# Cluster labels from one product per tile, with the halves added on VectorE, and new planner prices for column-tiled products

## The chip, the cores and the metric

The kernel runs on one core of a Trainium2 chip. The metric is the device time of one execution in microseconds (us): the median of the runs. One more execution was taken by the hardware profiler. The engines are called as in the profile: PE (TensorE's products), PEld (its weight loads), DVE (VectorE), ACT (ScalarE), POOL (GpSimd) and SP (SyncE, which issues the DMAs).

## The reference

Clustered attention over 4 batches, 8 heads, 768 positions and 64 dimensions, followed by a feed-forward layer. Each query and each key gets the label of the nearest of 16 centroids of its head (the largest cosine), and a query sees only keys of its own label:

```python
q_assign = np.argmax(np.einsum('bhsd,hcd->bhsc', q_n, c_n), axis=-1)
k_assign = np.argmax(np.einsum('bhsd,hcd->bhsc', k_n, c_n), axis=-1)
mask = q_assign[:, :, :, None] == k_assign[:, :, None, :]
scores = np.where(mask, scale * np.matmul(q, k.transpose(0, 1, 3, 2)), -1000000000.0)
attn = softmax(scores)
x = (attn @ v).transpose(0, 2, 1, 3).reshape(B * S, H * D)
h = x @ w_in
g = np.where(h >= 1, h, np.where(h <= -1, 0.0, (h + 1) ** 2 / 4))
out = g @ w_out
```

The feed-forward layer is 512 to 2048 to 512. All data are float32.

## The kernel before, in words

**Numbers.** To keep float32 accuracy with float16 products, every operand is split into a high and a low half that are both float16. A product of two such operands then takes three products (high with high, high with low, low with high), or, where one operand is stored with both halves side by side along the contraction, fewer. The rows of q and k are such: 64 dimensions with two halves fill the 128 rows of the array, so one weight tile of q or k holds both halves of 128 positions.

**Stages.** The work is cut into 12 units (`NU`): 4 batches (b) by 3 chunks (c) of 256 query positions. Heads go in 4 pairs (hp). Per batch and pair, `kv_load`, `k_scale`, `k_split`, `v_split` and `k_assign` load k and v, split them and find the keys' labels (12 tiles of 128 keys). Per unit, `q_load`, `q_scale`, `q_split`, `q_assign` and `q_pairs` do the same for q (16 tiles). Then `at_scores`, `at_soft` and `at_av` compute the attention of each pair, and `ffn1` and `ffn2` the feed-forward layer of the unit, in 8 slices f of 256 hidden columns. Slices of the weights are prepared in the first part of the kernel (`w_load`, `w_bits`, `w_split`).

**Labels.** `labels` (line 653) multiplies each tile of 128 positions (the weights, `xT[:, i]`) with the 16 centroids of its head. The centroids too are split into two halves, in `cT[:, a]`, so there are two products of 16 columns for each tile, and the second adds onto the first in PSUM: 32 products for a q unit, 24 for a pair of k. Then VectorE, all on that PSUM bank: the maximum over the 16, `is_equal` with it, times `iota`, the maximum again. The callers subtract that maximum: a zero marks the label.

**Memory.** PSUM has two pairs of banks, of which the scores use `pair[0]` alone once the start is over (`early()`: step under `EARLY` = 22), and `ffn2` the other. `bank_a` belongs to `at_av`. The three banks h, i, j go round in a ring (`hid`, `misc`) among `ffn1`, the labels and all small sums.

**Order.** The order of the instructions isn't written out. Each step of a stage calls a `Recorder`, which collects nodes (one instruction, or a group of products) with what they read and write. `price` (line 87) gives each a cost in ns, `turns` (line 119) says which VectorE and GpSimd instructions must not overlap, and `issue` (line 305) plans `ROUNDS` = 80 orders by list scheduling forwards and backwards. Each is replayed by a model of the machine in four phases of the clock gate, and the order with the smallest sum is issued. The steps (`at(step, fn, ...)`, line 1209 on) only set the recording order and first priorities: unit u begins at step 16u, `q_assign` comes 4.5 steps before it, `k_assign` of batch b and pair hp at step 48b + 4hp - 4 (6 before, for the first batch), `v_split` one step before that. So a change of any price can change the order of everything.

**Column-tiled products.** `at_av` (line 978) uses weight tiles of 64 columns, so that two heads share the array: 8 products of 128 columns for the row sums and 36 of 256 for the values, in one group. `price` calls them `half`: `n / 4.8 + 3.5` ns for n columns. Other products are `max(n / 2.4 + 2.5, 24)`.

Of the kernel before, what the change touches and what calls it, by code (L numbers as in the profile page):

```python
# [12 lines left out]
F32 = mybir.dt.float32  # L13
U32 = mybir.dt.uint32
AF = mybir.ActivationFunctionType
ALU = mybir.AluOpType
AX = mybir.AxisListType
# [25 lines left out]

LOOK, MARGIN = 0.4, 4000
ROUNDS = 80

class Recorder:
# [9 lines left out]
    def __init__(self, tc):  # L59
        self.tc, self.nc = tc, tc.nc  # L60
        self.nodes, self.seen, self.open, self.step = [], {}, None, -99
        for name in ("tensor", "scalar", "vector", "gpsimd", "sync"):
            setattr(self, name, Engine(self, name, getattr(tc.nc, name)))

# [22 lines left out]
    def price(self, eng, op, out, ins, kw):  # L87

        if "dma" in op:
            n = 1  # L90
            for k in out.shape:
                n *= k
            kb = n * mybir.dt.size(out.dtype) / 1024

            return 33, 79.0 if kb == 2 else kb, "transpose" in op
        n = max(self.free(a) for a in [out] + ins[:1])
        ps = any(a.space == PSUM for a in ins)
        cols = sum(isinstance(kw.get(k), bass.AP) for k in ("scale", "bias", "scalar", "scalar1", "scalar2"))
        if eng == "tensor":
            n = self.free(ins[1])  # L100
            half = self.free(ins[0]) <= 64 and n > 100
            if ins[1].dtype == F32:
                n *= 4

            return n / 4.8 + 3.5 if half else max(n / 2.4 + 2.5, 24)
        if eng == "scalar":
            cols += kw.get("accum_out") is not None
            first = n == 1 and kw.get("scale") == 0.0

            apart = n > 512 and any(list(a.ap)[-1][0] == 2 and mybir.dt.size(a.dtype) == 4 for a in [out] + ins[:1])  # L110
            return 93 + n / 1.2 + 94 * cols - 43 * ps + 1283 * first + 75 * apart
        if eng == "vector":
            fast = 1
            if op in ("tensor_scalar", "tensor_copy") and not ps:
                fast = 4 if mybir.dt.size(out.dtype) == 2 and mybir.dt.size(ins[0].dtype) == 2 and n > 64 else 2
            return 68 + n / 0.96 / fast + 61 * cols + 20 * (op == "reciprocal")
        return (150 if n < 16 else 55) + n * (2.03 if op == "tensor_tensor" else 0.9 if op == "memset" else 3.5)
# [187 lines left out]
    def issue(self):  # L305
# [4 lines left out]
        best = None  # L310
        for _ in range(ROUNDS):
            self.forward(prio)
# [83 lines left out]
class Group:  # L396
# [8 lines left out]
        r.nodes.append(r.open)  # L405

    def __exit__(self, *a):
        self.rec.open = None


class Engine:
# [22 lines left out]
def view(buf, shape, dtype):  # L434
    n = 1
    for k in shape:
        n *= k
    ap = buf.bitcast(dtype)[:, :n]
    if len(shape) > 1:
        names = "abcd"[: len(shape)]  # L440
        ap = ap.rearrange(
            "p (" + " ".join(names) + ") -> p " + " ".join(names), **dict(zip(names[1:], shape[1:]))
        )
    return ap
# [3 lines left out]
def tile_clustered_attention_moe(  # L448
# [12 lines left out]
    C = cent.shape[1]  # L461
# [5 lines left out]
    T = S // P  # L467
    NP = H // 2
    CT = 2
# [19 lines left out]
    rec = Recorder(tc)  # L489
# [4 lines left out]
    def tiles(name, n, size):  # L494
        return [const.tile([P, size // 4], U32, name=f"{name}{i}") for i in range(n)]

    def new(tag, shape, dtype, n=1):

        if tag not in rings:
            size = mybir.dt.size(dtype)  # L500
            for k in shape:
                size *= k
            rings[tag] = Ring(tiles(tag, n, -(-size // 32) * 32))
        return rings[tag](*shape, dtype=dtype)
# [26 lines left out]
    start = iter([0, 1] * 2).__next__  # L531

    def early():

        return rec.step < EARLY

    def misc(*shape):
        return hid(*shape, dtype=F32)
# [24 lines left out]
    cT = const.tile([P, 2, P], F16, name="cT")  # L563
# [69 lines left out]
    def transpose(out, nat, ps=None):  # L633
        nat = nat.rearrange("p n a d -> p (n a d)")
        if ps is None:
            rec.sync.dma_start_transpose(out=out, in_=nat)
            return

        n = out.shape[1] // 2
        ps = view(ps, [2, 4 * 256], BF16)  # L640
        nat, out = nat.bitcast(BF16), out.bitcast(BF16).rearrange("p (x n) q -> p x (n q)", x=2)
        for x in range(2):
            with rec.group():
                for i in range(n):
                    rec.tensor.transpose(ps[:, x, i * P : (i + 1) * P], nat[:, (x * n + i) * P : (x * n + i + 1) * P], idb)
            rec.scalar.copy(out[:, x], ps[:, x, : n * P])
# [3 lines left out]
        rec.scalar.activation(out=hi, in_=src, func=AF.Copy, scale=sc)  # L650
        rec.vector.scalar_tensor_tensor(out=lo, in0=src, scalar=sc, in1=hi, op0=ALU.mult, op1=ALU.subtract)

    def labels(z1, xT, n, heads):

        with rec.group():
            for i in range(n):
                for a in range(2):
                    h = heads[i]
                    rec.tensor.matmul(
                        z1[:, i], xT[:, i], cT[:, a, h * C : (h + 1) * C], start=(a == 0), stop=(a == 1)  # L660
                    )
        mx = new("mx", [NP * SC], F32)[:, :n]

        def wide(x):
            return x.unsqueeze(2).to_broadcast([P, n, C])

        rec.vector.tensor_reduce(out=mx, in_=z1, op=ALU.max, axis=AX.X)
        rec.vector.tensor_tensor(out=z1, in0=z1, in1=wide(mx), op=ALU.is_equal)
        rec.vector.tensor_tensor(out=z1, in0=z1, in1=iota.unsqueeze(1).to_broadcast([P, n, C]), op=ALU.mult)
        rec.vector.tensor_reduce(out=mx, in_=z1, op=ALU.max, axis=AX.X)  # L670
        return wide(mx)

    def kv_load(b, hp):
        slot = slots[hp]
# [47 lines left out]
    def k_assign(b, hp):  # L722

        e = KV[b, hp]
        n = 2 * T
        z1 = misc(n, C)
        kn = e["kn"]
        mx = labels(z1, e["kT"], n, [2 * hp + i // T for i in range(n)])
        rec.vector.tensor_tensor(out=z1, in0=z1, in1=mx, op=ALU.subtract)
        rec.gpsimd.memset(kn[:, :, 1, C:], 0.0)  # L730
        rec.vector.tensor_scalar(
            out=kn[:, :, 1, :C], in0=z1, scalar1=0.0, scalar2=-ONE, op0=ALU.not_equal, op1=ALU.mult
        )
        e["k1"] = view(e["parts"][1 if b == 0 else 2], [n, P], F16)
        transpose(e["k1"], kn, pair[start()] if b == hp == 0 else None)

        pn = misc(2, C)
        with rec.group():
            for t in range(T):
                rec.tensor.matmul(pn, ones, kn[:, t::T, 1, :C], start=(t == 0), stop=(t == T - 1))  # L740
        rec.vector.tensor_scalar(
            out=BX[b]["has"][:, hp], in0=pn, scalar1=-ONE * (S - 0.5), scalar2=None, op0=ALU.is_gt
        )

    Q = {}
    NQ = NP * SC
# [32 lines left out]

    def q_assign(u):  # L780
        e = Q[u]
        z1 = misc(NQ, C)
        mx = labels(z1, e["qT"], NQ, [i // CT for i in range(NQ)])
        zs = e["z"] = new("zs", [NQ, C], F32)
        rec.vector.tensor_tensor(out=zs, in0=z1, in1=mx, op=ALU.subtract)
        e["er"] = new("er", [NQ], F32, 2)

# [431 lines left out]
    for b in range(B):  # L1219
# [11 lines left out]
        for c in range(NCH):  # L1231
            u = b * NCH + c
            s0 = first(b, 0, c)
            for x, fn in zip((PRO, -9.1, -8.1, -6.1) if u == 0 else (s0 - 14, s0 - 6.8, s0 - 6.4, s0 - 4.5), (q_load, q_scale, q_split, q_assign)):
                at(x, fn, u)
            for hp in range(0, NP, NP if c else 1):
                at(first(b, hp, c) - (5.5 if u == 0 else 3), q_pairs, u, hp, NP if c else 1)
            for hp in range(NP):
                s0 = first(b, hp, c)
                for n in range(SC):  # L1240
                    at(s0 + n, at_scores, b, hp, c, n // CT, n % CT)
                    at(s0 + n + 1, at_soft, b, hp, c, n // CT, n % CT)
                at(s0 + LA - 0.5, at_av, b, hp, c)

            sf = max(sf, s0 + FA)
            G = NF if u else GF
            for f in range(NF):
                if f % G == 0 and (u < 2 or c == 0):
                    if u == 0:
                        sf = max(sf, wat[2 * (f + G) - 1] + 2)  # L1250
                    at(sf - 1, ffn_scale, [u] if u == 0 else range(u, (b + 1) * NCH), range(f, f + G))
                at(sf, ffn1, u, f)
                at(sf + 3, ffn2, u, f)
                sf += 2
    for i in range(2 * NF):
        f, a = divmod(i, 2)
# [47 lines left out]
```

## Time and profile before

| | |
|---|---|
| median of 3 runs | 867.04 us (865.24 to 868.2) |
| the profiled execution: its time | 869.13 us |
| its span, first to last instruction | 867.30 us |
| mean granted clock of TensorE | 0.984 |
| instructions | 19633 |

The profile's page lists, for each engine, its busy time, its share of the span and its number of instructions. The chain that ended last is followed back from the last instruction, at each step to what released it. A group of instructions is a line with engine, operation, out<-in by the program's names (bank numbers and buffer numbers left out), partitions x elements, count, busy us, mean ns of one, and after the bar the idle time of the engine just ahead of them and what ended it. All instructions have the recorder's line 322, so one goes by the names: `cT` are the centroids, `kn` and `n` the natural k, `bankh`, `banki`, `bankj` the ring of banks, `zs` the labels of q, `sS` the scores, `hl` their halves, `r` and `g` the hidden layer. A timeline line is start, length, engine, product or operation, and how many were merged. Products overlap in the array, and their ends are modelled, so the time from start to start is what one costs.

### The profile page before, as it was taken

To read this page: it belongs to the slowest core of one execution; us is meant where nothing else is said; L and a number is where in the kernel's file an instruction comes from. 1 tells how busy PE (TensorE), PEld (TensorE's weight loads), DVE (VectorE), ACT (ScalarE), POOL (GpSimd) and SP (SyncE) were. 2 spreads that over 40 slices of the span, in tenths; PEclk is the share of its full clock that TensorE was granted. 3 is DMA by queue.
4 is the path that set the end of the run, shared out by engine and by line. 5 is a ranking of instruction groups with operands and counts; after the bars stand their busy time and mean duration, and the time that the engine had idled before them with its cause. 6 is when DMAs were issued, how large, how long until landed. Compare 5 with 4: busy or idle time off the path is not lost.

```text
span 867.3 us, 19633 instructions
## 1 busy us (share of the span) xinstructions
PE 809.4 (93%) x7452; PEld 561.1 (65%) x7452; DVE 650.4 (75%) x1485; ACT 637.4 (73%) x1128; POOL 550.1 (63%) x527
## 2 busy tenths in 40 slices
PE   3687559999999999999999999999999999999997
PEld 3454346666767766767666766767667667676664
DVE  7999999998978868678778768678887757544322
ACT  6799888986867778678777687686776687676232
POOL 1166688876756777756766677666667577666222
PEclk9998889999999999999999999999999999999999
DMA  9985689869999979988998978998999787666100
GB/s 315 241 248 146 171 204 204 147 140 162 197 169 199 168 151 177 192 185 190 183 189 173 169 141 173 198 161 167 177 216 162 141 160 131 113 135 109 20 25 25
DMA packets 404767, 142.55 MB, mean 164 GB/s; under 512 B 372800, under 2 KB 396352, under 8 KB 404672
## 3 DMA queue, kind: packets, MB, share of 16 engines
q1 hardware_dynamic: 404672, 141.30, 80.2%
q8 instruction: 58, 0.95, 0.5%
q14 instruction: 37, 0.30, 0.1%
HBM read 40.40 MB, written 6.29 MB: 54 GB/s over the span
## 4 chain that ended last, share of the span: by engine, by line
PE 80%; DVE 12%; ACT 3%; issue 2%; DMA 2%; POOL 0%; ACTq 0%; SPq 0%; DVEq 0%; POOLq 0%
PE pair L322 40%; PE banka L322 11%; PE bankj L322 10%; PE banki L322 9%; PE bankh L322 9%; DVE sS L322 2%; DVE w L322 2%; DVE wk L322 1%; ACT w L322 1%; DMA q<-qn 1%; ACT hl L322 1%; DVE banki L322 1%; DVE qn L322 1%; ACT sS L322 1%; DVE q L322 1%
## 5 line engine op out<-in xcount | busy, mean ns | idle before, releaser
L322 POOL TENSOR_TENSOR hl<-sS,hl 128x768 f16<-128x768 f32 x176 | 299.8, 1711 | 116.0 <-ACT hl L322 83.7
L322 PE MATMUL pair<-w,g 128*128 128x512 f16 x1152 | 271.1, 379 | 0.0
L322 PEld LDWEIGHTS <-w 128*128 128x128 f16 x2304 | 223.4, 98 | 44.3 <-issue 2.6
L322 ACT ACTIVATE sS<-sS,sbi 128x768 f32<-128x768 f32 x192 | 179.3, 934 | 91.9 <-DVE sbi L322 88.6
L322 DVE CUSTOM_DVE_ANT_0 sS<-pair,zero,er 128x768 f32<-128x768 f32 x192 | 194.2, 1011 | 66.4 <-PE pair L322 41.6
L322 PEld LDWEIGHTS <-g 128*128 128x128 f16 x1152 | 110.3, 98 | 116.3 <-issue 1.6
L322 PE MATMUL pair<-kv,q 128*128 128x384 f16 x768 | 160.9, 334 | 17.6 <-DVE sbi L322 9.2
L322 ACT CAST hl<-sS 128x768 f16<-128x768 f32 x176 | 143.8, 825 | 12.9 <-DMA pT<-hl 7.9
L322 POOL TENSOR_TENSOR g<-r,g 128x512 f16<-128x512 f32 x88 | 103.7, 1179 | 63.7 <-ACT g L322 53.8
L322 PEld LDWEIGHTS <-q 128*128 128x128 f16 x1152 | 84.1, 99 | 72.8 <-issue 26.1
L322 PE MATMUL banka<-pT,kv 128*64 128x256 f16 (+1 forms) x1680 | 107.2, 282 | 0.4 <-DMA pT<-hl 0.4
L322 ACT ACTIVATE r<-r,f_ra,f_rs 128x512 f32<-128x512 f32 x88 | 71.3, 811 | 43.3 <-DVE r L322 42.5
L322 PEld LDWEIGHTS <-kv 128*64 128x64 f16 (+1 forms) x1968 | 96.9, 108 | 2.9 <-issue 1.5
L322 ACT CAST g<-r 128x512 f16<-128x512 f32 x88 | 53.8, 611 | 13.1 <-DVE r L322 10.2
L322 PE MATMUL bankh<-x,w 128*128 128x256 f16 x432 | 51.9, 273 | 0.2 <-POOL x L322 0.2
L322 POOL TENSOR_TENSOR qn<-qn,phi 128x256 f16<-128x256 f16 x48 | 34.2, 731 | 27.1 <-DVE phi L322 17.5
L322 PE MATMUL bankj<-x,w 128*128 128x256 f16 x408 | 48.3, 273 | 0.0
L322 PE MATMUL banki<-x,w 128*128 128x256 f16 x312 | 38.0, 273 | 0.0
L322 POOL TENSOR_TENSOR w<-w 128x1024 f16<-128x1024 f32 x12 | 30.2, 2513 | 10.6 <-ACT w L322 9.3
L322 PE MATMUL banki<-wk,w 128*128 128x256 f16 x312 | 36.7, 273 | 0.0
L322 ACT ACTIVATION_READ_ACCUMULATOR sS<-sS,sbi 128x1 f32 x192 | 36.0, 188 | 0.0
L322 PEld LDWEIGHTS <-ones 128*128 128x128 bf16 x256 | 18.0, 105 | 27.2 <-issue 21.6
(238 smaller groups left out, 1069.0 us busy)
## 6 DMA issues: line engine op xcount, KB each, us to landing
w<-in_moe_w_out_dram SPq DMA_DIRECT2D x14, 512.0 KB, 4.4
q<-in_q_dram SPq DMA_DIRECT2D x12, 512.0 KB, 4.9
kv<-in_k_dram SPq DMA_DIRECT2D x16, 384.0 KB, 3.8
kv<-in_v_dram SPq DMA_DIRECT2D x16, 384.0 KB, 4.4
out_dram<-o SPq DMA_DIRECT2D x11, 512.0 KB, 3.3
w<-in_moe_w_in_dram SPq DMA_DIRECT2D x10, 512.0 KB, 5.6
word<-in_moe_w_in_dram SPq DMA_DIRECT2D x6, 512.0 KB, 4.6
o<-in_v_dram SPq DMA_DIRECT2D x8, 384.0 KB, 4.5
```

Of the source, the lines that this page charges most:

```text
L322: fn(*args, **kw)
```

## The change

From step 22 on, `labels` multiplies each tile once with both halves of the centroids: 32 columns, which land side by side in PSUM (`z1[:, i]`, shape 2 x 16). A `tensor_reduce` on VectorE adds the two halves of each centroid into SBUF: for k into the third part of the pair's slot (where v was staged and the transposed labels go later), for q into `zs`. The first maximum and the first input of `is_equal` are read from there; `is_equal` writes to PSUM as before. Before step 22 nothing changes in `labels`.

The planner's prices change for the whole kernel: a column-tiled product costs `n / 4.8`, and a group that has any costs 248 ns more; the smallest price of another product is 25.2 instead of 24 ns.

```diff
+TILED = 248
...
+        self.tiled = False
...
-            return n / 4.8 + 3.5 if half else max(n / 2.4 + 2.5, 24)
+            self.tiled |= half
+            return n / 4.8 if half else max(n / 2.4 + 2.5, 25.2)
...
     def __exit__(self, *a):
-        self.rec.open = None
+        self.rec.open.cost += TILED * self.rec.tiled
+        self.rec.open, self.rec.tiled = None, False
...
-    def labels(z1, xT, n, heads):
-
+    def labels(xT, n, heads, tmp):
+
+        both = not early()
+        z1 = misc(n, 1 + both, C)
         with rec.group():
             for i in range(n):
+                h = heads[i]
+                if both:
+                    rec.tensor.matmul(z1[:, i], xT[:, i], cT[:, :, h * C : (h + 1) * C], start=True, stop=True)
+                    continue
                 for a in range(2):
-                    h = heads[i]
                     rec.tensor.matmul(
-                        z1[:, i], xT[:, i], cT[:, a, h * C : (h + 1) * C], start=(a == 0), stop=(a == 1)
+                        z1[:, i, 0], xT[:, i], cT[:, a, h * C : (h + 1) * C], start=(a == 0), stop=(a == 1)
                     )
         mx = new("mx", [NP * SC], F32)[:, :n]
+        zz, z1 = z1, z1[:, :, 0]
+        z = tmp if both else z1
+        if both:
+            rec.vector.tensor_reduce(out=z, in_=zz.rearrange("p n a c -> p n c a"), op=ALU.add, axis=AX.X)
...
-        rec.vector.tensor_reduce(out=mx, in_=z1, op=ALU.max, axis=AX.X)
-        rec.vector.tensor_tensor(out=z1, in0=z1, in1=wide(mx), op=ALU.is_equal)
+        rec.vector.tensor_reduce(out=mx, in_=z, op=ALU.max, axis=AX.X)
+        rec.vector.tensor_tensor(out=z1, in0=z, in1=wide(mx), op=ALU.is_equal)
...
-        return wide(mx)
+        return z1, wide(mx)
...
-        z1 = misc(n, C)
         kn = e["kn"]
-        mx = labels(z1, e["kT"], n, [2 * hp + i // T for i in range(n)])
+        z1, mx = labels(e["kT"], n, [2 * hp + i // T for i in range(n)], view(e["parts"][2], [n, C], F32))
...
-        z1 = misc(NQ, C)
-        mx = labels(z1, e["qT"], NQ, [i // CT for i in range(NQ)])
         zs = e["z"] = new("zs", [NQ, C], F32)
+        z1, mx = labels(e["qT"], NQ, [i // CT for i in range(NQ)], zs)
         rec.vector.tensor_tensor(out=zs, in0=z1, in1=mx, op=ALU.subtract)
```

## The prediction

> **What bounds the kernel now.** I read the page's busy times first, then the busy time by stretches, then who waited for whom, and only then the groups. The page (busy us, share of the span, instructions; then the head of the chain that ended last):
>
> ```profile
> PE 809.4 (93%) x7452; PEld 561.1 (65%) x7452; DVE 650.4 (75%) x1485; ACT 637.4 (73%) x1128; POOL 550.1 (63%) x527
> PE 80%; DVE 12%; ACT 3%; issue 2%; DMA 2%; POOL 0%; ACTq 0%; SPq 0%; DVEq 0%; POOLq 0%
> ```
>
> An average of 93% hides two stages. The busy time in three stretches (columns: length, PE, PEld, DVE, ACT, POOL, granted clock, DMA share, GB/s):
>
> ```profile
> 0.00:210.00 210.00, 156.59 (x1462) 108.45 (x1463) 194.22 (x455) 174.81 (x287) 132.97 (x130) 0.93 0.83 200
> 210.00:860.00 650.00, 650.00 (x5980) 451.62 (x5979) 456.14 (x1031) 461.35 (x840) 417.14 (x397) 1.00 0.81 154
> 860.00:867.30 7.30, 2.78 (x13) 1.08 (x11) 0.00 (x0) 1.27 (x2) 0.00 (x0) 0.96 0.19 72
> ```
>
> In the opening 210 us TensorE lacks work for 210 - 156.59 = 53.4 us and VectorE is busy 194.22 of 210: there VectorE and ScalarE set the pace. From 210 to 860 us TensorE is busy for 650.00 of 650 at granted clock 1.00. What TensorE waited for says the same, from 200 us to the end (one line is all there is), and over the whole span the longest two:
>
> ```profile
> PE bankj L322 <- DMA q<-qn: 0.6, 1, 0.6
> ```
>
> ```profile
> PE pair L322 <- ACT sS L322: 10.7, 9, 3.8
> PE pair L322 <- DVE sbi L322: 9.2, 6, 5.7
> ```
>
> So after 210 us every product that goes away should end the kernel sooner by its issue time, as long as the other engines keep feeding; in the opening it should not.
>
> **The products removed.** The change only acts from step 22 on. The label products after 100 us, by bank (count: duration min/median/max, first to last start):
>
> ```profile
> L322 PE MATMUL banki<-cT,q x128: 169/169/173, 136.8 to 726.4; 128*128 128x16 f16 x128
> L322 PE MATMUL bankj<-cT,q x96: 169/169/183, 203.3 to 526.5; 128*128 128x16 f16 x96
> L322 PE MATMUL bankh<-cT,kv x96: 169/169/173, 206.1 to 257.2; 128*128 128x16 f16 x96
> L322 PE MATMUL bankh<-cT,q x96: 169/169/173, 280.6 to 585.2; 128*128 128x16 f16 x96
> L322 PE MATMUL bankj<-cT,kv x96: 169/169/183, 397.5 to 455.7; 128*128 128x16 f16 x96
> L322 PE MATMUL banki<-cT,kv x96: 169/169/183, 588.9 to 644.2; 128*128 128x16 f16 x96
> ```
>
> That is 320 products on q, 10 groups of 32 (units 2 to 11: unit 2's q_assign has step 32 - 4.5 = 27.5), and 288 on k, 12 groups of 24 (batches 1 to 3). All are past step 22, so each group loses half: 160 + 144 = 304 products, with a weight load each. The 169 ns is no price, because products overlap; the price is from start to start. TensorE's timeline, three places (start, length, product, count):
>
> ```profile
> 280.64 0.95 PE L322 MATMUL bankh<-cT,q 128*128 128x16 f16 x32
> 281.45 1.46 PE L322 MATMUL pair<-w,g 128*128 128x512 f16 x6
> ```
>
> ```profile
> 643.61 0.75 PE L322 MATMUL banki<-cT,kv 128*128 128x16 f16 x24
> 644.21 0.81 PE L322 MATMUL pair<-kv,q 128*128 128x384 f16 x4
> ```
>
> ```profile
> 405.11 0.30 PE L322 MATMUL bankh<-n,ones 128*128 128x32 f16 x6
> 405.26 0.81 PE L322 MATMUL pair<-kv,q 128*128 128x384 f16 x4
> ```
>
> 32 products take 0.81 us (25.3 ns each), 24 take 0.60 us (25.0 ns), and six products of 32 columns take 0.15 us (25 ns): at these widths the number of products counts and not their columns. So a product with both halves should cost 25.2 ns too, and the saving is 304 x 25.2 ns = 7.66 us. The group at 136.8 us (16 products fewer, 0.40 us) lies in the opening, where TensorE waits anyway; I leave it out: 7.26 us. Bounds: none of it, if a 32-column product with new weights each time costs twice as much (a rival below), and 7.66 us.
>
> **The work added to VectorE.** Each of the 22 groups gets one sum from PSUM over 512 (q) or 384 (k) elements. The nearest rows are the maxima over 256 and 192, from the groups of instructions with shapes apart, with three rows of a tensor_tensor whose inputs both lie in SBUF:
>
> ```profile
> L322 DVE TENSOR_REDUCE mx<-bankh 128x16 f32<-128x256 f32 x10 | 4.2, 417 | 0.8 <-PE bankh L322 0.7
> L322 DVE TENSOR_REDUCE mx<-bankh 128x12 f32<-128x192 f32 x10 | 3.5, 355 | 1.4 <-PE bankh L322 1.2
> L322 DVE TENSOR_TENSOR banki<-zs,has 128x256 f32<-128x256 f32 x4 | 3.0, 756 | 0.0
> L322 DVE TENSOR_TENSOR bankj<-zs,has 128x256 f32<-128x256 f32 x2 | 1.4, 694 | 0.0
> L322 DVE TENSOR_TENSOR bankh<-zs,has 128x256 f32<-128x256 f32 x2 | 0.8, 419 | 0.0
> L322 DVE TENSOR_TENSOR bankh<-bankh,mx 128x256 f32<-128x256 f32 x5 | 2.1, 428 | 0.1
> ```
>
> 64 elements more cost 62 ns, 0.97 ns each, so I estimate 417 + 256 x 0.97 = 665 ns and 355 + 192 x 0.97 = 541 ns: 10 x 0.665 + 12 x 0.541 = 13.1 us. The sum reads with a stride of 16 elements, which no row shows; twice that, 26 us, is my upper end, and 13.1 us my value, because the maxima are the same instruction on the same memory. Then is_equal gets its first input from SBUF instead of PSUM, beside the maxima in SBUF. With one input in PSUM it takes 428 ns; the rows with two inputs in SBUF take from 419 to 756, (3.0 + 1.4 + 0.8) / 8 = 0.65 us on average, long whenever GpSimd is at work. That is +0.22 us, 22 times: 4.9 us, between nothing and 22 x 0.33 = 7.2. All in all 18 us.
>
> The Trainium skill, SBUF - State Buffer, "Who interferes with whom", says that such an instruction and a GpSimd one that reads SBUF share a port pair and that the later one blocks until the first ends. The spread of the rows agrees that there is a conflict. By full blocking behind GpSimd's costliest form a single wait could reach some 1.7 us (the page's first group):
>
> ```profile
> L322 POOL TENSOR_TENSOR hl<-sS,hl 128x768 f16<-128x768 f32 x176 | 299.8, 1711 | 116.0 <-ACT hl L322 83.7
> ```
>
> Taken 22 times that would be 38 us in the place of 4.9; the rows above stay under 0.4 us each, so they give the sum.
>
> What hides the 18 us: from 210 to 860 VectorE is idle for 650 - 456.14 = 194 us. Queued behind the new sum is above all the score eviction, whose end frees the only score buffer. One label chain on VectorE's timeline:
>
> ```profile
> 393.88 0.41 DVE L322 TENSOR_REDUCE mx<-banki 128x16 f32<-128x256 f32 x1
> 394.57 1.02 DVE L322 CUSTOM_DVE_ANT_0 sS<-pair,zero,er 128x768 f32<-128x768 f32 x1 [0.28 <-PE pair L322]
> 395.51 0.08 DVE L322 DVE_READ_ACCUMULATOR2_ANT sbi<- 128x1 f32 x1
> 395.51 0.43 DVE L322 TENSOR_TENSOR banki<-banki,mx 128x256 f32<-128x256 f32 x1
> ```
>
> The chain already sits in pieces between evictions, and VectorE even waits for TensorE there. A sum of 0.67 us where 0.28 are free would push this eviction by 0.4 us; TensorE's fixed order has feed-forward products between score groups, and it waited 0.6 us in all after 200 us. So I take nothing on TensorE's path. If that cover went, the 18 us would be its price (a rival).
>
> **The added dependency.** For k the sums go to the part of the slot in which v was staged, so the sum must wait for v_split's reads. In the trace one v_split ends after the labels of its pair have begun (batch 2, first pair):
>
> ```profile
> 398.89 0.35 DVE L322 TENSOR_REDUCE mx<-bankj 128x12 f32<-128x192 f32 x1
> 404.22 1.00 DVE L322 SCALAR_TENSOR_TENSOR kv<-kv,sv 128x768 f16<-128x768 f32 x1
> ```
>
> The planner has to turn them round: that moves 1.0 us of VectorE ahead of the labels, or holds the labels' bank 5 us longer. Two other banks stay for the feed-forward meanwhile. I take nothing, with 1 us for this pair as the other end. For q the target zs is written earlier in the same chain; its last reader belongs to the unit before. No DMA is added and nothing is moved past on SP or GpSimd by hand.
>
> **The new prices.** They change no instruction but may change the whole issue order. An attention-value group (8 and 36 column-tiled products) is charged 8 x 30.2 + 36 x 56.8 = 2.29 us before and 8 x 26.7 + 36 x 53.3 + 248 = 2.38 us after. Measured, from the timeline:
>
> ```profile
> 282.84 0.41 PE L322 MATMUL banka<-idu,rr 128*64 128x128 f16 x8
> 283.09 2.13 PE L322 MATMUL banka<-pT,kv 128*64 128x256 f16 x36
> 285.15 0.82 PE L322 MATMUL pair<-kv,q 128*128 128x384 f16 x4
> ...
> 290.39 1.46 PE L322 MATMUL pair<-w,g 128*128 128x512 f16 x6
> 291.69 0.81 PE L322 MATMUL pair<-kv,q 128*128 128x384 f16 x4
> ```
>
> The group takes 285.15 - 282.84 = 2.31 us. The six products ahead of it, begun at 281.45, took 1.39 us until it started, where six of the same kind with an untiled follower take 291.69 - 290.39 = 1.30. With this 0.09 us the group costs 2.40 us, and the new price is the nearer one. After 210 us any order that feeds TensorE ends at the same time; only the 53.4 us of gaps in the opening can grow or shrink. The trace cannot show the new order. My value is zero, and my bounds one stall as long as the longest behind VectorE there (5.7 us) more or less.
>
> **Sum.** The profiled execution took 869.13 us, 1.83 beyond its span of 867.30, and lies 2.09 above the median of 867.04. 869.13 - 7.26 + 0 + 0 = 861.9 for a profiled execution like it; against the median, 867.04 - 7.26 = **859.8 us**, 0.84% less.
>
> **The rivals.**
> *The opening gets worse (slower).* The new prices redraw the order in the opening, where weight preparation, q and k splits and score evictions compete for VectorE. A score group's wait for VectorE cost 5.7 us there once. From 9.9 us of extra waiting on (7.26 + 2.6) the kernel is measurably slower; two such stalls more give 859.8 + 11.4 = 871.2 us. For: VectorE is 92% busy there. Against: nearly all of the removed and added work comes later. Chance 0.07.
> *VectorE becomes the bound (slower).* If the label chains set the pace after 210 us, halved products are worth nothing and 18 us come on top: 885 us. It decides once a chain's extra 0.8 us can't be absorbed between two score groups. For: 75% busy on average. Against: 194 idle us. The Trainium skill's Perfetto Trace Analysis, "Identifying the Most-Contended Engine", gives this case weight: it distrusts TensorE's matmul busy share and judges it by its weight loads, 65% here, under VectorE's 75%, so VectorE would count as the engine to relieve. The trace disagrees: start-to-start times without waits after 210 us. Chance 0.02.
> *The products aren't cheaper (the change doesn't do what it says).* A 32-column product with new weights takes 50 ns, so groups last as long as before: 867 us. Against: the six at 405.11, though all with one weight tile; and groups in which every second load brings new weights average 25 ns. Chance 0.04.
> *Part of the gain is given back* in the opening or at the turned-round pairs, between 4.7 and 9.9 us: about 867 us. Chance 0.07.
>
> **How the numbers follow.** About 0.3% (2.6 us) is what a measurement of this kernel can tell from no change; the three runs span 865.24 to 868.2. The forecast has chance 0.80; its own range is 859.8 with 5.7 us to each side, 854.1 to 865.5. To hold most of the unchanged cases I widen the upper end to 867.0; beyond lie the two slower rivals. Faster 0.80, same 0.04 + 0.07 = 0.11, slower 0.07 + 0.02 = 0.09.
>
> **What would show it.** TensorE with 7452 - 304 = 7148 products; label groups from step 22 on with 16 and 12 products, 0.40 and 0.30 us to the next start; 22 new VectorE reductions near 665 and 541 ns; is_equal near 0.65 us; TensorE still busy throughout from about 210 us to the end; gaps in the opening of 53 us, give or take 6. It would be wrong if waits of TensorE on VectorE or on labels show after 210 us, if the opening's gaps change by over 6 us, or if a group with half the products lasts as long as before.

## The result, and the profile after

The kernel after takes 871.54 us (median of 7 runs, 870.08 to 875.18), against 867.91 us for the kernel before (7 runs, 865.24 to 870.1): ratio 1.0046, 95% interval 1.0026 to 1.0066. It is 3.6 us slower, where 7.3 us less were forecast. The profiled execution took 871.23 us.

The page's busy times and the chain that ended last, of the kernel after:

```profile
PE 809.9 (93%) x7148; PEld 558.0 (64%) x7148; DVE 675.5 (78%) x1507; ACT 636.2 (73%) x1128; POOL 544.4 (63%) x527
PE 65%; DVE 12%; ACT 4%; DMA 3%; issue 3%; POOL 2%; ACTq 0%; POOLq 0%; DVEq 0%
```

The 304 products are gone and VectorE has 22 instructions and 25 us more. TensorE's share of the chain fell from 80 to 65%: the chain now leaves TensorE more often. The label groups on TensorE's timeline cost what was forecast, 0.41 and 0.30 us to the next start:

```profile
478.87 0.56 PE L325 MATMUL bankj<-cT,q 128*128 128x32 f16 x16
479.28 0.81 PE L325 MATMUL pair<-kv,q 128*128 128x384 f16 x4
...
647.50 0.46 PE L325 MATMUL banki<-cT,kv 128*128 128x32 f16 x12
647.80 0.81 PE L325 MATMUL bankh<-x,w 128*128 128x256 f16 x6
```

VectorE's groups with shapes apart: of the sums one row for q and one for k, then is_equal, whose inputs now both lie in SBUF, all six rows:

```profile
L325 DVE TENSOR_REDUCE zs<-banki 128x256 f32<-128x512 f32 x4 | 2.7, 684 | 0.6 <-PE banki L325 0.6
L325 DVE TENSOR_REDUCE kv<-bankj 128x192 f32<-128x384 f32 x4 | 2.2, 552 | 3.0 <-PE bankj L325 3.0
L325 DVE TENSOR_TENSOR banki<-zs,mx 128x256 f32<-128x256 f32 x4 | 5.1, 1275 | 0.1
L325 DVE TENSOR_TENSOR bankh<-zs,mx 128x256 f32<-128x256 f32 x3 | 2.8, 929 | 0.0
L325 DVE TENSOR_TENSOR bankj<-zs,mx 128x256 f32<-128x256 f32 x3 | 1.7, 559 | 0.0
L325 DVE TENSOR_TENSOR bankj<-kv,mx 128x192 f32<-128x192 f32 x4 | 3.1, 782 | 0.1
L325 DVE TENSOR_TENSOR banki<-kv,mx 128x192 f32<-128x192 f32 x4 | 2.5, 631 | 0.0
L325 DVE TENSOR_TENSOR bankh<-kv,mx 128x192 f32<-128x192 f32 x4 | 1.5, 364 | 0.1
```

The sums are right (684 and 552 ns; 665 and 541 forecast). is_equal takes 9.6 us on q and 7.1 us on k, where the old rows (428 ns and about 365) would make 8.7 together: 8.0 us more, over the 7.2 that were my upper end. Why some of them are so long is seen on the timelines of VectorE and GpSimd (POOL), at two of the q groups:

```profile
288.39 1.64 POOL L325 TENSOR_TENSOR hl<-sS,hl 128x768 f16<-128x768 f32 x1
288.78 1.54 DVE L325 TENSOR_TENSOR bankh<-zs,mx 128x256 f32<-128x256 f32 x1
```

```profile
482.95 0.42 DVE L325 TENSOR_TENSOR bankj<-zs,mx 128x256 f32<-128x256 f32 x1
483.12 1.75 POOL L325 TENSOR_TENSOR hl<-sS,hl 128x768 f16<-128x768 f32 x1 [0.24 <-DMA pT<-hl]
```

The is_equal that begins during a GpSimd instruction ends 0.29 us after it (290.32 against 290.03 us); the one that begins first takes its 0.42 us. The stretches (same columns as before), and all that TensorE waited for after 210 us:

```profile
0.00:210.00 210.00, 161.45 (x1429) 112.01 (x1429) 195.47 (x459) 174.76 (x286) 126.86 (x128) 0.89 0.83 202
210.00:860.00 650.00, 643.54 (x5699) 443.98 (x5698) 480.02 (x1049) 459.71 (x841) 416.43 (x399) 1.00 0.81 153
860.00:869.40 9.40, 4.94 (x23) 2.06 (x21) 0.00 (x0) 1.73 (x3) 1.15 (x1) 0.90 0.15 56
```

```profile
PE pair L325 <- DVE sbi L325: 2.4, 3, 0.9
PE bankh L325 <- DVE n L325: 1.7, 1, 1.7
PE pair L325 <- DMA q<-qn: 0.8, 1, 0.8
PE banki L325 <- POOL word L325: 0.5, 1, 0.5
PE pair L325 <- ACT o L325: 0.3, 1, 0.3
PE bankj L325 <- DVE zs L325: 0.2, 1, 0.2
```

Here is the answer to the question where the time went: the full stretch after 210 us isn't full any more. TensorE idles for 6.5 us, mostly behind VectorE (4.3 of the 5.9 us listed). In the opening it is busier than before, but at a lower clock (0.89 against 0.93), so busy times don't compare there. I therefore counted the work by starts: every product at n / 2.4 + 2.5 ns for n columns (at least 25.2; float32 columns count four times), column-tiled ones at n / 4.8, and set the sum against the clock on the wall. The "loss" of a stretch is its length less the work issued in it. After 210 us about 10.5 us of loss are in every kernel with this work: the switches into, within and out of the 39 column-tiled groups there (0.09 + 0.03 + 0.15 us each).

| us | all work | loss to 210 | loss 210 to 850 | span |
|---|---|---|---|---|
| before | 793.1 | 58.4 | 11.1 | 867.3 |
| after | 785.4 | 58.8 | 20.5 | 869.4 |
| difference | -7.7 | +0.4 | +9.4 | +2.1 |

So TensorE issues 7.7 us less work, as forecast, and loses 9.4 us more after 210 us. One such wait, on the timeline of the kernel after (in brackets the idle time and what ended it):

```profile
437.97 0.37 DVE L325 TENSOR_TENSOR bankj<-bankj,iota 128x192 f32<-128x192 f32 x1
438.25 1.01 DVE L325 CUSTOM_DVE_ANT_0 sS<-pair,zero,er 128x768 f32<-128x768 f32 x1
...
439.97 0.36 DVE L325 TENSOR_SCALAR n<-bankj 128x192 f16<-128x192 f32 x1
...
440.38 0.30 PE L325 MATMUL bankh<-n,ones 128*128 128x32 f16 x6 [1.70 <-DVE n L325]
```

The end of a label chain of k (`n`, the one-hot labels) comes 1.7 us late for six tiny products that TensorE's fixed order has put there, and everything behind them waits. The same order with the old labels (a run below) waits 0.4 us at this place: the order has the hole there, and most of its size comes with the labels (with the halved products alone, 1.2 us).

### The profile page after: what moved, and what is told of

Its sections match the earlier page's. It is cut to its first block, busy times and chain, and to the rows that moved or that the text cites. A ratio compares the mean times of both kernels' runs of the same rounds, so it can differ in the third digit from the quotient of the medians.

```text
span 869.4 us, 19068 instructions
## 1 busy us (share of the span) xinstructions
PE 809.9 (93%) x7148; PEld 558.0 (64%) x7148; DVE 675.5 (78%) x1507; ACT 636.2 (73%) x1128; POOL 544.4 (63%) x527
## 4 chain that ended last, share of the span: by engine, by line
PE 65%; DVE 12%; ACT 4%; DMA 3%; issue 3%; POOL 2%; ACTq 0%; POOLq 0%; DVEq 0%
PE pair L325 32%; PE banka L325 9%; PE bankh L325 9%; PE banki L325 8%; PE bankj L325 8%; DVE sS L325 3%; DMA pT<-hl 2%; DVE r L325 2%; POOL hl L325 2%; DVE qn L325 1%; ACT sS L325 1%; ACT hl L325 1%; DVE wk L325 1%; ACT r L325 1%; DVE bankh L325 1%
## 5 line engine op out<-in xcount | busy, mean ns | idle before, releaser
L325 POOL TENSOR_TENSOR hl<-sS,hl 128x768 f16<-128x768 f32 x176 | 295.2, 1684 | 81.6 <-ACT hl L325 70.2
L325 PE MATMUL pair<-kv,q 128*128 128x384 f16 x768 | 162.7, 336 | 20.2 <-DVE sbi L325 11.4
L325 POOL TENSOR_TENSOR g<-r,g 128x512 f16<-128x512 f32 x88 | 105.9, 1203 | 92.5 <-ACT g L325 86.4
L325 ACT CAST hl<-sS 128x768 f16<-128x768 f32 x176 | 144.6, 826 | 11.6 <-DMA pT<-hl 9.9
L325 PEld LDWEIGHTS <-q 128*128 128x128 f16 x992 | 80.2, 99 | 76.8 <-issue 33.5
L325 PEld LDWEIGHTS <-kv 128*64 128x64 f16 (+1 forms) x1824 | 92.6, 109 | 2.9 <-issue 1.6
L325 POOL CAST rr<-rs 128x4 f16<-128x4 f32 x48 | 14.1, 295 | 36.9 <-DVE rs L325 35.9
```

The lines of the kernel that those rows point to most:

```text
L325: fn(*args, **kw)
```

## The experiments

Theory A: the new issue order costs, and the labels themselves save about 7 us. Theory B: the longer label chain on VectorE costs. The sharpest test keeps an order. The planner still plans with the instructions of the one kernel, and then the instructions inside the same nodes are exchanged; the sequence of nodes on every engine stays as it was. What it can't keep is the timing that the planner had in mind: `turns` set VectorE's and GpSimd's instructions apart for the durations that were planned. In the headings, the median and the ratio to the kernel before on the same chip.

**Old order, products halved, sum left out (861.69 us; 0.9929, 0.9917 to 0.9942).** The labels from step 22 on come from the high halves alone, so this is the price of the products and nothing else.

```diff
+        if not early():
+            group, first, equal = rec.nodes[k0 : k0 + 3]
+            zz = view(hid.last(), [2, n, C], F32)
+            zi = zz.rearrange("p a n c -> p n a c")
+            group.calls = [
+                (nc.tensor.matmul, (zi[:, i], xT[:, i], cT[:, :, heads[i] * C : (heads[i] + 1) * C]), dict(start=True, stop=True))
+                for i in range(n)
+            ]
```

> The issue order of the kernel before, node for node, with only the products halved from step 22 on: 16 or 12 products of 32 columns, the two halves in two blocks of the bank. The sum is left out, so the labels there come from the high halves alone, and VectorE's chain is as before. Both theories, A (the order) and B (the label chain), expect the products' price here: 867.7 - 7.3 = 860.4 us, 859 to 862. If it stays at 866 or more, products are not what TensorE's time after 210 us is made of.

It saved 868.35 - 861.69 = 6.7 us, near the 7.3 of the forecast. All that TensorE waited for after 210 us, in this run:

```profile
PE banki L322 <- DVE zs L322: 0.4, 1, 0.4
```

With TensorE's stretch full, a product that goes away is time that goes away. This step of the prediction is shown, for this order.

**Old order, new labels (882.60 us; 1.0169, 1.0156 to 1.0182).** As above, and the first maximum's node issues the sum ahead of the maximum; is_equal reads the sum. The sum of k goes to a tile of its own.

```diff
+            first.calls = [
+                (nc.vector.tensor_reduce, (), dict(out=z, in_=zz.rearrange("p n a c -> p n c a"), op=ALU.add, axis=AX.X)),
+                (nc.vector.tensor_reduce, (), dict(out=mx, in_=z, op=ALU.max, axis=AX.X)),
+            ]
+            equal.calls = [(nc.vector.tensor_tensor, (), dict(out=z1, in0=z, in1=wide(mx), op=ALU.is_equal))]
```

> The issue order of the kernel before, node for node, with the new labels put in: from step 22 on a label group issues 16 or 12 products of 32 columns, and the node of the first maximum issues the sum and then the maximum (the sum of k goes to a small tile of its own, that of q to the tile of q's labels). Theory A (the new issue order is what costs: TensorE lost about 10 us to its own waits, while halved groups took 0.40 and 0.30 us as forecast): 868 - 7 = 861 us, 859 to 864. Theory B (the longer label chain on VectorE costs: sums of 684 and 552 ns, and is_equal stretched by GpSimd to as much as 1.5 us): no gain, 868 to 872 us, with waits of TensorE on VectorE after 210 us.

Neither theory's number: 15 us slower, worse than B expected. TensorE's waits after 210 us, the longest:

```profile
PE pair L322 <- DVE sbi L322: 4.2, 5, 1.7
PE banki L322 <- DVE zs L322: 2.6, 1, 2.6
PE bankh L322 <- DVE zs L322: 2.5, 1, 2.5
PE bankj L322 <- DVE zs L322: 1.7, 1, 1.7
```

**Old order, new labels, first maximum in PSUM (873.85 us; 1.0060, 1.0045 to 1.0075).** is_equal then has one input in SBUF and one in PSUM. Against the run before this one, the edit is:

```diff
+            mp = view(hid.last(), [2, n * C], F32)[:, 1, :n]
...
-                (nc.vector.tensor_reduce, (), dict(out=mx, in_=z, op=ALU.max, axis=AX.X)),
+                (nc.vector.tensor_reduce, (), dict(out=mp, in_=z, op=ALU.max, axis=AX.X)),
...
-            equal.calls = [(nc.vector.tensor_tensor, (), dict(out=z1, in0=z, in1=wide(mx), op=ALU.is_equal))]
+            equal.calls = [(nc.vector.tensor_tensor, (), dict(out=z1, in0=z, in1=wide(mp), op=ALU.is_equal))]
```

> As the run of the new labels in the old order (882.6 us), but the first maximum goes to PSUM, so that is_equal has one input in SBUF and one in PSUM. The sum stays. If the waits for GpSimd in is_equal are what the old order could not take (8 us of VectorE in the profile of the kernel after), 868 to 874 us; if it is the sum's own 13 us that come unplanned, 878 to 883 us.

The costliest is_equal row of the run before this one, and the same instruction here:

```profile
L322 DVE TENSOR_TENSOR banki<-zs,mx 128x256 f32<-128x256 f32 x4 | 5.1, 1275 | 0.0
```

```profile
L322 DVE TENSOR_TENSOR banki<-zs,banki 128x256 f32<-128x256 f32 x4 | 1.7, 423 | 0.0
```

One input out of SBUF takes the instruction from 1275 back to 423 ns, and the kernel from 882.6 to 873.9 us: the conflict with GpSimd cost the kernel 8.7 us (9.4 if each run is taken from the kernel before on its own chip). Over all 22, is_equal takes 17.9 us in the one run and 8.5 in the other, so of 9.4 us of VectorE hardly any was hidden. The Trainium skill's SBUF - State Buffer, "Who interferes with whom", says that a VectorE instruction with two SBUF inputs contends with a GpSimd one that reads SBUF, and that one with at most one such input, outside the modes that use both port pairs, does not; these two rows agree. What is left over the run with halved products is 873.85 - 861.69 = 12.2 us. All of it comes with the sum, but not as its 13 us one for one. TensorE's costliest waits after 210 us in this run:

```profile
PE bankh L322 <- DVE zs L322: 2.4, 1, 2.4
PE banki L322 <- DVE zs L322: 2.0, 1, 2.0
PE bankj L322 <- DVE zs L322: 1.7, 1, 1.7
```

They end with the last instruction of a label chain of q (`zs`), which gives the bank back to the next feed-forward products; behind the score evictions (`pair` <- `sbi`) TensorE waits only 0.3 us. Besides, VectorE is busy 18.9 us longer than with the halved products (665.4 against 646.5), more than the sums, which take 13.4: shifted by them, 48 instructions `q<-q,phi` take 32.6 us in place of 28.4, one ahead of the first wait 1.75 us beside GpSimd instead of 0.34. And twice the granted clock fell to 0.50 for 3.4 us (the column after POOL), about 1 us after the first of these waits ended and right after the second:

```profile
287.70:291.10 3.40, 3.40 (x18) 2.37 (x16) 2.12 (x6) 2.56 (x5) 2.32 (x2) 0.50 1.10 114
676.80:680.20 3.40, 3.40 (x15) 1.95 (x13) 2.17 (x6) 1.97 (x4) 0.73 (x1) 0.50 0.45 86
```

At half the clock that is 3.4 us of the 12.2; with the halved products alone the clock is 1.00 from 210 to 850 us. The run before this one has two such stretches as well, so the 8.7 us are free of them. That the waits set them off isn't shown: other waits of 1.7 us (the third of these, and the one at 440.38 us in the kernel after) had no such stretch behind them. In an order that didn't foresee them, VectorE's 194 idle us hid next to nothing: B is right for this order.

**New order, three times.** The order of the kernel after, node for node, with the old labels (877.12 us; 1.0113, 1.0096 to 1.0131), with halved products and the sum left out (872.96; 1.0056, 1.0038 to 1.0074), and with the new labels and the first maximum in PSUM (870.26; 1.0028, 1.0013 to 1.0043).

```diff
+        if both:
+            group, add, first, equal = rec.nodes[k0 : k0 + 4]
+            group.calls = [
+                (
+                    nc.tensor.matmul,
+                    (z1[:, i], xT[:, i], cT[:, a, heads[i] * C : (heads[i] + 1) * C]),
+                    dict(start=(a == 0), stop=(a == 1)),
+                )
+                for i in range(n)
+                for a in range(2)
+            ]
+            add.calls = []
+            first.calls = [(nc.vector.tensor_reduce, (), dict(out=mx, in_=z1, op=ALU.max, axis=AX.X))]
+            equal.calls = [(nc.vector.tensor_tensor, (), dict(out=z1, in0=z1, in1=wide(mx), op=ALU.is_equal))]
```

This is the first, which puts the old 32 or 24 products back. The second has the same edit without `group.calls`. The third changes only where the first maximum goes:

```diff
+            m1 = zz[:, 0, 1, :n]
+            first.calls = [(nc.vector.tensor_reduce, (), dict(out=m1, in_=z, op=ALU.max, axis=AX.X))]
+            equal.calls = [(nc.vector.tensor_tensor, (), dict(out=z1, in0=z, in1=wide(m1), op=ALU.is_equal))]
```

> The issue order of the kernel after, node for node, with the old labels put in: 32 or 24 products of 16 columns, no sum, is_equal with one input in PSUM. Theory A (order): the products come back on top of the bad order, 871.5 + 7 = 878 us, 875 to 880. Theory B (label chain): VectorE is relieved of 21 us, so TensorE's waits after 210 us go: 871.5 + 7.3 - 6.5 = 872 us or less.

> The issue order of the kernel after, node for node, with halved products and without the sum, which is left out (the labels from step 22 on come from the high halves alone), is_equal with one input in PSUM. With the old labels this order takes 877.1 us. The products alone: 877.1 - 7 = 870 us. If the sum and the port conflict cost TensorE little in an order that was planned for them, the kernel after (871.5) is at most 2 us above this; if they cost as much as in the old order (21 us), this would have to be near 851 us.

> The issue order of the kernel after, node for node, with the first maximum in PSUM, so that is_equal has one input in SBUF. If the port conflict costs TensorE anything in this order, faster than 871.5 by that: 867 to 870 us. If not, 871 to 873 us.

With the old labels in both, the new order takes 877.1 and the old one, on the same chip, 867.7: **with the old labels the new order costs 9.4 us**. The labels, in the new order, go from 877.1 to 871.5: **there they save 5.6 us**. Together that is about the result, +3.6. But the two can't be priced apart: the other way round, the labels in the old order cost 14.9 us and the new order then takes 11 of them back. An order fits the instructions that it was planned for; 9.4 us are the price of this one for instructions that it wasn't planned for, and VectorE is busy 660.0 us in that run against 650.4 before, without any new work.

Of the 5.6 us, the halved products give 877.12 - 872.96 = 4.2, not 6.7 as in the old order: by starts the loss after 210 us rises from 17.7 to 20.6 us, so part of the time that the products set free is spent waiting. Leaving out the sum and its conflict gains nothing over the kernel after (872.96 against 871.54); taking away the conflict alone perhaps 1.3 us, within the intervals. The first of these isn't as clean as it looks. Some 21 us of VectorE's work are left out, but VectorE is busy only 11.6 us less (663.9 against 675.5). The costliest reason, in the kernel after and then in the run with the halved products:

```profile
L325 DVE TENSOR_SCALAR q<-q,phi 128x512 f16<-128x512 f16 x48 | 29.3, 615 | 0.1
```

```profile
L325 DVE TENSOR_SCALAR q<-q,phi 128x512 f16<-128x512 f16 x48 | 36.6, 767 | 0.1
```

The stretch after 210 us, of the new order with the old labels and then with the halved products:

```profile
210.00:860.00 650.00, 645.34 (x5936) 447.66 (x5935) 463.67 (x1031) 459.03 (x840) 415.96 (x399) 1.00 0.81 153
```

```profile
210.00:860.00 650.00, 643.04 (x5699) 443.89 (x5698) 468.94 (x1031) 459.95 (x841) 415.96 (x399) 1.00 0.82 153
```

Neither is full, though neither has a sum. So the sums aren't needed for the holes of this order, and A holds as far as that. That an order planned with the sums in it hides them altogether isn't shown, since these two runs have instructions that the order didn't foresee. What an order costs with the work that it was planned for, the redraws below tell.

**Prices alone, labels alone.** The kernel before with the new prices (878.06 us; 1.0118, 1.0105 to 1.0131), and the kernel after with the old prices (875.88; 1.0091, 1.0075 to 1.0106). The edits are the pieces of the change's diff that touch the planner, and those from `labels` on.

> The kernel before with the new prices alone (column-tiled products and the smallest product), labels as before. Theory A: a new order from nothing but prices; the time moves by several us, and to the slower side if the prices are at fault: 871 to 880 us. Theory B: the prices change nothing that matters, 867 to 870 us.

> The kernel after with the old prices, so the new labels alone, planned anew. Theory A: any new plan is a draw around the old one, less 7 us for the products: 858 to 870 us, and most likely faster than the kernel after. Theory B: the label chain costs as in the kernel after, 870 to 873 us.

The prices alone, planned anew, cost 10 us without adding or removing an instruction. But the labels alone are slow as well, with the old prices. Are the prices bad, or is any new order?

**The same kernel, drawn again.** One planner constant is changed by an amount that has no meaning; the work, the labels and the prices stay, and only the order changes.

```diff
-AHEAD = 1500
+AHEAD = 1501
```

The others change `TURN_WAIT` from 200 to 201, `SLACK` from 20 to 21 or `MARGIN` from 4000 to 4100.

> The kernel before, with one planner constant changed without meaning (AHEAD from 1500 to 1501): prices and labels as before, a new issue order. Theory A (the order before is a tight draw, and almost any other loses some us to waits of TensorE): 871 to 878 us. Theory A2 (the new prices themselves lead to worse orders): 866 to 869 us, as before.

> The kernel before, drawn again (TURN_WAIT 201). A third order with the same work and prices: 868 to 876 us if draws spread by several us, 867 to 871 us if the old prices give tight orders as a rule.

> The kernel before, drawn a fourth time (SLACK 21). If the order before is a tight draw, 870 to 876 us; if the two other draws were bad luck, 866 to 869 us.

> The kernel after, with one planner constant changed without meaning (TURN_WAIT from 200 to 201): a new issue order. Theory A: another draw, somewhere from 864 to 876 us, apart from the kernel after by over 2 us in the one or the other direction. Theory A2: 870 to 873 us, as the kernel after.

> The kernel after, drawn a third time (MARGIN 4100). Draws so far 871.5 and 873.8: 868 to 878 us; under 864 would show that the forecast's gain is there for a good order.

> The old labels with the new prices, drawn again (TURN_WAIT 201). If the 10 us of the run with the prices alone were bad luck, 867 to 873 us; if the new prices lead to worse orders by themselves, 875 to 881 us again.

| labels, prices | draws, us (ratio to the kernel before on the same chip) |
|---|---|
| old, old | 867.91; 870.66 (1.0027); 873.64 (1.0065); 881.49 (1.0151) |
| old, new | 878.06 (1.0118); 871.65 (1.0040) |
| new, old | 875.88 (1.0091) |
| new, new | 871.54 (1.0046); 873.83 (1.0077); 876.54 (1.0097) |

A meaningless digit costs the kernel before 2.3, 5.7 and 14.0 us against the kernel before on the same chip. The kernel before is the fastest of its four draws (the mean of the four is 873.4), and the kernel after is the fastest of its three (mean 874.0). With so few draws, spread so widely, it stays open whether the labels gain or lose anything on average once the planner is free. The new prices, drawn twice, lie within the old prices' draws, so that they are worse by themselves isn't shown. The third redraw, TensorE's two stretches and its costliest wait after 210 us:

```profile
0.00:210.00 210.00, 155.28 (x1425) 107.37 (x1426) 190.89 (x445) 169.47 (x277) 123.66 (x125) 0.90 0.79 192
210.00:860.00 650.00, 644.46 (x5930) 446.41 (x5928) 464.49 (x1035) 462.41 (x843) 418.70 (x399) 1.00 0.82 157
```

```profile
PE pair L322 <- DVE sbi L322: 3.2, 6, 1.1
```

It idles after 210 us as the kernel after does (5.5 us against 6.5), with the old labels and the old prices: a draw of the order is enough for such holes, and no sum is needed. By starts it loses 5.5 us more than the kernel before in the opening and 7.7 us more from 210 to 850.

**No conflict, planned anew.** The new labels with the first maximum in PSUM, in which the planner, too, sees one input in PSUM; with the old prices (and `TURN_WAIT` 201; 872.83 us; 1.0055, 1.0035 to 1.0075) and with the new ones (and `MARGIN` 4100; 867.27; 0.9989, 0.9977 to 1.0001).

```diff
-        zz, z1 = z1, z1[:, :, 0]
+        zz, z1 = z1, view(hid.last(), [n, C], F32)
+        m1 = view(hid.last(), [2, n * C], F32)[:, 1, :n] if both else mx
...
-        rec.vector.tensor_reduce(out=mx, in_=z, op=ALU.max, axis=AX.X)
-        rec.vector.tensor_tensor(out=z1, in0=z, in1=wide(mx), op=ALU.is_equal)
+        rec.vector.tensor_reduce(out=m1, in_=z, op=ALU.max, axis=AX.X)
+        rec.vector.tensor_tensor(out=z1, in0=z, in1=wide(m1), op=ALU.is_equal)
```

> The new labels with the first maximum in PSUM, so that is_equal no longer has both inputs in SBUF, the prices of the kernel before, planned anew (with TURN_WAIT 201, one of several draws). If the label chain's own cost is what ate the products' gain, taking the port away gives some of it back: 862 to 869 us. If the draw of the order rules, it lies where the other draws lie: 870 to 876 us.

> The same labels with the new prices, planned anew (with MARGIN 4100). If the new prices lead to worse orders by themselves, this lies over the run with the old prices, 871 to 877 us; if they are harmless, within 2 us of it.

The second is level with the kernel before and the best version of the new labels. The two differ by 5.6 us, in the other direction than "the new prices are worse" would have it. That is within the width of a draw, so neither proves anything about the port; the two runs in the old order, which differ in the port alone, do that.

## Why the prediction was wrong, point by point

- **What bounds the kernel**: right for the kernel before. TensorE's start-to-start time after 210 us is that kernel's time: 7.3 us of products taken out of a full stretch gave 6.7. In the new order, whose stretch isn't full, they gave 4.2.
- **The products**: right, in number, in price and, in the old order, in effect. That they wouldn't get cheaper (a rival) is refuted by the groups of 0.41 and 0.30 us.
- **The sums**: right in duration. "What hides the 18 us: from 210 to 860 VectorE is idle for ... 194 us" fails in the old order: 12.2 us came with the sum's 13 (3.4 of them by the clock) and 8.7 with the conflict's 9.4. What counts is the idle time ahead of the instruction that TensorE waits for, and not the total. And that instruction was above all the end of the label chain itself, whose bank the feed-forward needed ("Two other banks stay for the feed-forward meanwhile"): with the first maximum in PSUM, 6.1 of 8.0 us waited. The score eviction, which the prediction watched, made 0.3. How much of the 18 us a planned order hides isn't known.
- **The conflict**: is_equal cost 8.0 us more, not 4.9, in the kernel after. I took the mean of rows that were partly free of GpSimd. Single waits on q reached 1.1 us (1541 ns for 428), and the row of 1.54 us above shows the full blocking that the Trainium skill's SBUF - State Buffer, "Who interferes with whom", states. The 38 us for 22 waits of the longest kind would still have been far too much, since 11 of the 22 took at most 0.45 us.
- **The new order**: this is the step that failed. "My value is zero, and my bounds one stall as long as the longest behind VectorE there (5.7 us) more or less", with the reason "After 210 us any order that feeds TensorE ends at the same time; only the 53.4 us of gaps in the opening can grow or shrink". The second sentence begs the question: the new order doesn't feed TensorE all the time. The kernel after loses 9.4 us more after 210 us than the kernel before. The term was mis-sized: orders of the same work, with nothing but a digit changed, took 2.3 to 14.0 us longer, and the new order took 9.4 us longer with the old labels. In the profiled executions of that last pair, 7.7 us apart, the counting by starts puts 6.6 of it after 210 us (17.7 against 11.1) and 1.0 into the opening (59.4 against 58.4). The bound would have had to be about 14 us, and not even about zero: all nine other draws of the table came out slower than the kernel before, which was a lucky order.
- **The rivals**: the slower one put the loss into the opening, 9.9 us or more; it came after 210 us, and the opening lost 0.4 us more. That its time, 871.2 us, is close to the 871.5 measured is luck. "VectorE becomes the bound" gave 885 us, and the old order with the new labels came near it (882.6). In the kernel after VectorE doesn't set the pace: TensorE is busy 643.5 of the 650 us. The Trainium skill's Perfetto Trace Analysis, "Identifying the Most-Contended Engine", judges TensorE by two measures, MFU (the share of the peak rate that its products reach) and weight loads. The prediction used the weight loads alone, and by these (64%, against VectorE's 78%) VectorE would be the engine to relieve in the kernel after as well; it did not look at MFU.

What stays open: why this planner's orders differ so much in holes, which pair of nodes makes each hole, and how the 3.6 us divide between the draw and the longer label chain. That the order of the kernel before is an unusually tight one rests on four draws.

## What to carry to other kernels

Where a planner or a heuristic sets the order of everything, an edit has two effects, its own and that of a new draw, and the second can be larger: redraw the unchanged kernel a few times before reading anything into one per cent. To price the edit itself, keep the order and exchange the instructions inside it, and see from the other instructions' durations whether they kept theirs: here some collided with GpSimd that were planned not to. And a stretch without a single gap is not slack for later edits but the mark of an order that just fits: what is idle in total on another engine says little about what hides there.

## What the runs showed of the hardware

A tensor_tensor on VectorE with both inputs in SBUF took 0.42 us when it began before a GpSimd instruction, and ended 0.29 us after the GpSimd instruction when it began during one (1.54 us). Putting a maximum of 16 elements in PSUM was enough to undo it: from 813 to 388 ns on average over the 22, and from 1275 to 423 ns in the costliest bank. Short products of 128 rows cost 25 ns from start to start whether they have 16 or 32 columns, and whether the weights change with each or with every second.
